# A later output projection, and two copies moved behind a product, in the core of an attention gradient kernel

## The chip, the cores and the metric

The kernel runs on one core of a Trainium2 chip. The metric is the device time of one execution in microseconds (us). Two kernels are compared by the ratio of the mean times of their fast runs of the same rounds on the same chip, with a 95% interval; this is not quite the ratio of the medians that are quoted beside it. A profile is that of a single execution, so its span differs by a few us from the median.

The engines are named as in the profiles: in this kernel PE does the matrix products (PEld is its loading of weights), ACT exponentials and copies, DVE and POOL element-wise work, and SP only issues DMAs. PSUM is the memory, in banks, that PE's products go to. The *granted clock* is the share of PE's full clock that the chip allowed, as the profile records it.

## The reference, cut to what matters

The reference returns the output and all input gradients of two attention blocks side by side: A is linear attention, B is softmax attention with 16 query heads of width 28 and a single key and value head. Only B's core matters here (S = 2048, D = 448):

```python
q = (x @ wq).reshape(B, S, H, Dh).transpose(0, 2, 1, 3)
k = x @ wk
v = x @ wv
p = softmax(einsum("bhqd,bkd->bhqk", q, k) * Dh ** -0.5)
o = einsum("bhqk,bkd->bhqd", p, v)
out_B = o.transpose(0, 2, 1, 3).reshape(B, S, H * Dh) @ wo   # the output projection
# ... and jax.vjp of all of it
```

## The kernel before

B's core computes forward and backward in one loop of 540 *units*. A block is 8 units: 256 queries of 2 heads against all 2048 keys. Eight blocks, 64 units, are a *group*: all heads of 256 queries. The scores S of unit u are computed together with the gradient product of unit u-16; the output o of a block is ready 8 units after the block starts, dQ 26 units after. Each engine follows the program order below; `due(u, lag)` gives the block that started `lag` units ago. Names in the code and the profiles: eT is the exponential of S and eN its transpose, which the product dv reads; onat is o by rows and oTq its transpose, which the output projection reads; qX is the copy of q that the product dk reads; a *cast* is the copy of the projection out of PSUM into the buffer that is stored.

```python
for u in range(NU + 28):
    w = u - 16
    if u == 14 or u % 64 == 32 and u < 448:          # qX of the next group, 16 loads by SP
        ...
        for a in range(4):
            for B in range(4):
                r0 = qc * 256 + 64 * B
                nc.sync.dma_start(qx[32 * a:32 * a + 32, B, :, :],
                                  qn_d[r0:r0 + 64, :].rearrange("(j s) c -> j s c", s=2))
    ...
    rows_SD(u, sp, dp)                                # PE: S and dP, into PSUM
    ...                                               # PE: transposes of o and dO into a spare bank
    if u % 64 in (4, 12) and u > 64:
        out_proj(u, spare)                            # PE: 4 matmuls that read oTq
    ... # ACT: eT = exp(S), first half
    ... # DVE: dsT = dP * eT, first half (the gradient product); ACT copies, POOL multiplies the other
    if (b := due(u, 10)) is not None:
        o_norm(b)
        do_o(b)
        if b % 8 == 7:                                # u % 64 == 2: o of a whole group is ready
            q_ = b // 8
            oTq[q_] = pp_.tile([P, 8, P], BF16, name="oTq", bufs=1)
            nc.sync.dma_start_transpose(oTq[q_][:, :, :], onat[q_]...)
    if u % 64 in (4, 12) and u > 64:
        out_store(u, spare)                           # DVE cast, then a store by SP
    ... # ACT: eT, second half; every odd unit SP issues the DMA transpose eN <- eT
    ... # PE: dk products (odd units); o, dq and dv products (even units); dv reads eN
    ... # DVE: stream transpose dsx <- dsT, row sum row_D
    if (b := due(u, 8)) is not None:                  # copy of o
        oTs[b] = pm_.tile([64, 256], F32, name="oTs", bufs=1)
        nc.vector.tensor_copy(out=oTs[b][:, :], in_=oq[0:64, 0:256])
    if (b := due(u, 26)) is not None:                 # copy of dQ
        ... nc.vector.tensor_scalar(out=qT_B[g]..., in0=oq[64:128, 0:256], scalar1=scale, ...)
```

The store takes its row tile from one fixed place, so two stores of a group share one buffer:

```python
def out_store(u, ps):
    i = 2 * (u // 64 - 1) + u % 64 // 8
    ot = flat(R3)[:, 5120:5120 + D]
    nc.vector.tensor_copy(out=ot, in_=ps[:, 0:D])
    nc.sync.dma_start(out0[i * P:(i + 1) * P, D:2 * D], ot)
```

## Time and profile before

| | before |
|---|---|
| median of 4 runs | 1224.02 us (1221.16 to 1226.29) |
| span of the profiled execution | 1216.1 us |
| block of 8 units with nothing in the way | 12.26 us |
| block with the first projection, groups 1 to 7 | 28.21, 22.65, 22.90, 22.72, 24.68, 23.87, 23.05 us |
| block with the second projection | 13.0 us |
| SP's lag at unit 64q+19, groups 1 to 7 | 0.03 us, in group 5 0.08 |

Block times are differences of start times of the first exponential of successive blocks in the trace. *SP's lag* is the time from the end of the second exponential of an odd unit, which completes eT, to the moment SP starts to issue the DMA transpose of that eT. Both are worked out from the start times in the timeline.

The windows view gives the busy time of each engine in a stretch without projections. ACT's 39.42 of 40 us is the fullest; DVE and PE follow closely:

```profile
core 0: us, PE busy (x) PEld busy (x) DVE busy (x) ACT busy (x) POOL busy (x), PEclk, DMA share, GB/s
400.00:440.00 40.00, 37.84 (x696) 16.85 (x689) 38.09 (x73) 39.42 (x79) 32.94 (x37) 1.00 0.94 168
```

The list of waits names who waited for whom (us in total, times, longest). PE's wait for the DMA that fills oTq is the cause in these four lines; the others are the engines that PE then held up:

```profile
ACT eT L826 <- PE dps L591: 91.2, 23, 15.9
DVE R L636 <- issue: 74.6, 8, 14.3
PEld L79 <- DMA oTq<-onat: 71.7, 8, 13.7
PE sps L79 <- DMA oTq<-onat: 69.5, 8, 13.5
```

The timeline of SP, which issues these DMAs, at one such stop (start, duration, instructions). The columns show SP issuing eN transposes until 699.84, though o of the group (onat) was written by DVE at 694.07; only then come the store of onat, the transpose into oTq and, once PE and DVE have worked again, the store of the output at 706.84:

```profile
689.24 10.50 SPq L850 DMA_TRANSPOSE eN<-eT  x4
699.84 0.85 SPq L721 DMA_DIRECT2D on_d<-onat  x1
700.74 1.28 SPq L841 DMA_TRANSPOSE oTq<-onat  x1
702.13 2.30 SPq L850 DMA_TRANSPOSE eN<-eT  x1
706.84 0.36 SPq L637 DMA_DIRECT2D out_dram<-R  x1
```

The chain that ended last, by line, has the copy of dQ as "DVE R L897" with 2%:

```profile
PE dk_acc L591 15%; PE agen L79 10%; PE oq L591 8%; PE dps L591 7%; PE sps L591 7%; DVE dsT L831 6%; PE dv_acc L591 5%; PE sps L79 5%; ACT eT L847 4%; DVE dsx L887 3%; ACT eT L826 3%; PE aacc L79 3%; DMA oTq<-onat 3%; DVE R L897 2%; PE dps L79 2%
```

### The profile page before, as it was taken

How to read it: one execution, taken by the hardware profiler on the slowest of the kernel's cores; microseconds unless marked ns; L12 is line 12 of the kernel's file. 1: busy time of each engine (PE TensorE's matmuls, PEld its weight loads, DVE VectorE, ACT ScalarE, POOL GpSimd, SP SyncE). 2: the span in 40 equal slices, each digit the busy share in tenths (PEclk: the TensorE clock that was granted, in tenths of full speed). 3: DMA queues.
4: the chain of work that ended last, by engine and by line, in shares of the span. 5: the costliest groups of instructions: out<-in, count | busy, mean ns of one | idle time of the engine just before them, and what ended most of it. 6: DMA issues, size and time to landing. Idle time of an engine off the chain costs nothing.

```text
span 1216.1 us, 38536 instructions
## 1 busy us (share of the span) xinstructions
PE 1069.1 (88%) x15379; PEld 487.8 (40%) x15388; DVE 903.3 (74%) x1733; ACT 875.0 (72%) x1724; POOL 700.7 (58%) x835
## 2 busy tenths in 40 slices
PE   7999989888985996999699879969996997899798
PEld 3555544333432443444244334424442443344344
DVE  7885400437995997899699879959996997899732
ACT  3543212457994997899699969959996998799421
POOL 9000230005883886688588858857885787688710
PEclk9999998986997999999899989989998999999899
DMA  9679894099999999899999999999999999999972
GB/s 254 126 138 180 179 207 112 6 194 188 169 189 172 172 166 199 153 161 178 175 176 166 187 159 170 176 170 163 161 190 164 167 170 198 153 173 169 221 153 73
DMA packets 684437, 202.92 MB, mean 167 GB/s; under 512 B 651232, under 2 KB 679392, under 8 KB 684256
## 3 DMA queue, kind: packets, MB, share of 16 engines
q1 hardware_dynamic: 673664, 190.26, 89.9%
q10 hardware_dynamic: 9312, 6.65, 1.9%
q0 software_dynamic: 1280, 3.55, 1.0%
q8 instruction: 120, 1.97, 0.6%
q14 instruction: 61, 0.50, 0.1%
HBM read 22.83 MB, written 15.03 MB: 31 GB/s over the span
## 4 chain that ended last, share of the span: by engine, by line
PE 64%; DVE 17%; ACT 9%; DMA 5%; SPq 3%; issue 2%; POOL 0%; ACTq 0%; DVEq 0%; POOLq 0%
PE dk_acc L591 15%; PE agen L79 10%; PE oq L591 8%; PE dps L591 7%; PE sps L591 7%; DVE dsT L831 6%; PE dv_acc L591 5%; PE sps L79 5%; ACT eT L847 4%; DVE dsx L887 3%; ACT eT L826 3%; PE aacc L79 3%; DMA oTq<-onat 3%; DVE R L897 2%; PE dps L79 2%
## 5 line engine op out<-in xcount | busy, mean ns | idle before, releaser
L834 POOL TENSOR_TENSOR dsT<-cp,eT 128x512 bf16<-128x512 bf16 x512 | 591.9, 1156 | 241.6 <-ACT cp L833 232.2
L826 ACT ACTIVATE eT<-sps 128x512 bf16<-128x512 f32 x512 | 307.3, 600 | 114.9 <-PE dps L591 91.2
L831 DVE TENSOR_TENSOR dsT<-dps,eT 128x512 bf16<-128x512 f32 x512 | 350.3, 684 | 41.8 <-PE dps L591 33.3
L887 DVE STREAM_TRANSPOSE dsx<-dsT 128x512 f32<-128x512 f32 x512 | 357.4, 698 | 1.1
L591 PEld LDWEIGHTS <-R 32*128 32x128 bf16 (+1 forms) x8192 | 203.4, 94 | 324.8 <-issue 274.0
L833 ACT ACTIVATE cp<-dps 128x512 bf16<-128x512 f32 x512 | 304.6, 595 | 19.8 <-PE dps L591 19.8
L847 ACT ACTIVATE eT<-sps 128x512 bf16<-128x512 f32 x512 | 310.5, 606 | 0.0
L591 PE MATMUL dps<-doT,R 32*128 32x256 bf16 x2048 | 255.7, 273 | 15.7 <-DVE dsT L831 14.5
L591 PE MATMUL dk_acc<-dsx,qX 32*32 32x512 bf16 x4096 | 269.3, 377 | 0.0
L591 PE MATMUL sps<-R,R 32*128 32x256 bf16 x2048 | 246.6, 279 | 18.5 <-ACT eT L826 4.4
L591 PE MATMUL oq<-eT,R 128*32 128x256 bf16 x2048 | 163.0, 283 | 0.0
L591 PE MATMUL oq<-dsT,R 128*32 128x256 bf16 x2048 | 162.6, 282 | 0.0
L591 PEld LDWEIGHTS <-qX 32*32 32x32 bf16 x4096 | 80.0, 89 | 114.7 <-issue 54.4
L591 PE MATMUL dv_acc<-eN,don 128*32 128x512 bf16 x1024 | 84.1, 398 | 0.5 <-DMA eN<-eT 0.5
L79 PE MATMUL sps<-R,oTq 128*128 128x448 bf16 x64 | 20.8, 464 | 69.5 <-DMA oTq<-onat 69.5
L636 DVE CAST R<-sps 128x448 bf16<-128x448 f32 x16 | 10.0, 624 | 74.9 <-issue 74.6
L521 DVE TENSOR_TENSOR osb<-R 32x512 bf16<-32x512 bf16 x4 | 1.7, 414 | 72.4 <-ACT R L518 72.4
L380 POOL MEMSET ga<- 64x448 bf16 x2 | 0.9, 469 | 90.7 <-PE agen L337 71.3
L79 PEld LDWEIGHTS <-R 128*128 128x128 bf16 (+1 forms) x416 | 34.1, 99 | 36.3 <-issue 12.0
L553 POOL MEMSET R<- 128x16 bf16 x1 | 0.2, 175 | 70.2 <-DVE R L552 70.2
L719 POOL TENSOR_TENSOR don<-R,rl 128x128 bf16<-128x128 bf16 x64 | 26.0, 406 | 21.0 <-DVE rl L711 21.0
L79 PEld LDWEIGHTS <-oTq 128*128 128x128 bf16 x64 | 5.9, 114 | 78.4 <-DMA oTq<-onat 71.7
(203 smaller groups left out, 994.6 us busy)
## 6 DMA issues: line engine op xcount, KB each, us to landing
qX<-qn_d SPq DMA_DIRECT2D x128, 64.0 KB
out_dram<-osb ACTq DMA_DIRECT2D x44, 112.0 KB
eN<-eT SPq DMA_TRANSPOSE x256
qn_d<-dsx SPq DMA_DIRECT2D x1, 2048.0 KB
on_d<-onat SPq DMA_DIRECT2D x8, 256.0 KB
xa<-in_A_x_dram SPq DMA_DIRECT2D x8, 224.0 KB
ga<-in_grad_out_dram SPq DMA_DIRECT2D x4, 448.0 KB
xa<-in_grad_out_dram POOLq DMA_DIRECT2D x4, 448.0 KB, 5.0
```

Source lines behind the costliest of these rows:

```text
L79: nc.tensor.matmul(out_ap, lhsT=lhsT, rhs=rhs, start=start, stop=stop, tile_position=(0, 0))
L521: nc.vector.tensor_tensor(out=sq[0:32, :], in0=kT[0:32, qc * 512:(qc + 1) * 512], in1=kT[0:32, qc * 512:(qc + 1) * 512], op=ALU.mult)
L591: nc.tensor.matmul(out, lhsT=lhsT, rhs=rhs, start=start, stop=stop, tile_position=pos, skip_group_check=True)
L636: nc.vector.tensor_copy(out=ot, in_=ps[:, 0:D])
L719: nc.gpsimd.tensor_tensor(out=dn[:], in0=dnv, in1=r_[:].to_broadcast([P, 2, 2, 32]), op=ALU.mult)
L826: nc.scalar.activation(out=et[:, u % 2, 0, :], in_=sp[0][:, :], func=ACT.Exp, scale=scale)
L831: nc.vector.tensor_tensor(out=dst[:, 0, :], in0=dp[0][:, :], in1=ew[:, w % 2, 0, :], op=ALU.mult)
L833: nc.scalar.activation(out=cp[:, :], in_=dp[1][:, :], func=ACT.Copy)
L834: nc.gpsimd.tensor_tensor(out=dst[:, 1, :], in0=cp[:, :], in1=ew[:, w % 2, 1, :], op=ALU.mult)
L847: nc.scalar.activation(out=et[:, u % 2, 1, :], in_=sp[1][:, :], func=ACT.Exp, scale=scale)
L887: nc.vector.transpose(out=dsx[b][:, tp, :, :, :].rearrange("p h t c -> p (h t c)").bitcast(F32), in_=dsT[y][:, :, :].rearrange("p h c -> p ...
L897: nc.vector.tensor_scalar(out=qT_B[g][64 * hp:64 * hp + 64, qc * 256:(qc + 1) * 256], in0=oq[64:128, 0:256], scalar1=scale, scalar2=None, ...
```

## The change

The intent is to read oTq long after its DMA was issued, and to let the gradient product, for which PE waits, go ahead of two DVE copies.

```diff
-            i = 2 * (u // 64 - 1) + u % 64 // 8
+            i = 2 * (u // 64 - 1) + (u % 64 == 24)          # in out_proj and in out_store
...
-                if u % 64 in (4, 12) and u > 64:
+                if u % 64 in (20, 24) and u > 64:
                     out_proj(u, spare)
...  (behind the gradient product of unit u:)
+                if (b := due(u, 9)) is not None:
+                    oTs[b] = pm_.tile([64, 256], F32, name="oTs", bufs=1)
+                    nc.vector.tensor_copy(out=oTs[b][:, :], in_=oq[0:64, 0:256])
+                if (b := due(u, 27)) is not None:
+                    ... nc.vector.tensor_scalar(out=qT_B[g]..., in0=oq[64:128, 0:256], ...)
...
-                if u % 64 in (4, 12) and u > 64:
+                if u % 64 in (20, 24) and u > 64:
                     out_store(u, spare)
...  (at the end of the unit:)
-                if (b := due(u, 8)) is not None:
-                    ...
-                if (b := due(u, 26)) is not None:
-                    ...
```

The second store now follows the first by 4 units instead of 8.

More of the change, by code (lines that the diff above doesn't have):

```diff
@@ L633, in out_store @@
         def out_store(u, ps):
-            i = 2 * (u // 64 - 1) + u % 64 // 8
+            i = 2 * (u // 64 - 1) + (u % 64 == 24)
             ot = flat(R3)[:, 5120:5120 + D]
@@ L834 @@
                     nc.gpsimd.tensor_tensor(out=dst[:, 1, :], in0=cp[:, :], in1=ew[:, w % 2, 1, :], op=ALU.mult)
+                if (b := due(u, 9)) is not None:
+                    oTs[b] = pm_.tile([64, 256], F32, name="oTs", bufs=1)
+                    nc.vector.tensor_copy(out=oTs[b][:, :], in_=oq[0:64, 0:256])
+                if (b := due(u, 27)) is not None:
+                    qc, pair, g, hp = blk(b)
+                    nc.vector.tensor_scalar(out=qT_B[g][64 * hp:64 * hp + 64, qc * 256:(qc + 1) * 256],
+                                            in0=oq[64:128, 0:256], scalar1=scale, scalar2=None, op0=ALU.mult)
                 if (b := due(u, 10)) is not None:
@@ L891 @@
                     row_D(b)
-                if (b := due(u, 8)) is not None:
-                    oTs[b] = pm_.tile([64, 256], F32, name="oTs", bufs=1)
-                    nc.vector.tensor_copy(out=oTs[b][:, :], in_=oq[0:64, 0:256])
-                if (b := due(u, 26)) is not None:
-                    qc, pair, g, hp = blk(b)
-                    nc.vector.tensor_scalar(out=qT_B[g][64 * hp:64 * hp + 64, qc * 256:(qc + 1) * 256],
-                                            in0=oq[64:128, 0:256], scalar1=scale, scalar2=None, op0=ALU.mult)
         gwo(60, 64)
```

## The prediction

> **What bounds the kernel now.** 900 of the profiled 1216 us are B's core (250 to 1165 us): 64 blocks of 8 units. Between first exponentials of successive blocks I measure 12.26 us where nothing is in the way. There ACT is busy 98.5%, DVE 95%, PE 95% (windows view, 400 to 440 us): all three nearly bind. In each group of 64 units the block with the first output projection takes 22.65 to 28.2 us, the one with the second 13.0.
>
> oTq is transposed by DMA after unit 64q+2 and read by PE at 64q+4. The wait list gives PE 69.5 us on it in 8 waits; ACT's 91 us before its exponentials and DVE's 74.6 us before the projection's cast are the same stops. The transpose lands in 3.6 us; the rest is the queue: SP (timeline) is 4 to 11 us behind there, because the 16 qX loads at unit 64q+32 hold it up by 8.7 us and it catches up 0.26 us per eN transpose. After each stop the clock is 0.5 for some 4 us, as the Trainium skill, "TensorE: Matmul & The Clock Gate", Part 1, says of an idle PE.
>
> **What the change does.** No work is added. Projections go to units 20 and 24, 27 us after the transpose is issued; its wait should vanish. Excess of the first block of groups 1 to 7 over 12.26: 82 us. Projections that do not wait keep 0.75 us each (as unit 12 now), so at most 77 us, plus some 4 of the 5.1 us wait in the tail.
>
> The copies of o (0.38 us) and dQ (0.43 us; 2% of the chain) stand on DVE before the gradient product of units 1 and 3 (of 8). Moved behind it, product 3 comes 0.4 us earlier, but the copy and the row sum then precede product 4, which starts when it does now; DVE has no gap from unit 1 to 5. I expect 12.26 to stay within 0.1: 0 from this part.
>
> **What takes some back.** In the stops SP catches up (lag 0.03 us after each). Without them SP needs per 64 units about 32 x 2.8 (eN gap when behind) + 8.6 (qX) + 2.2 (on_d, oTq) + 1.8 (stores) = 100.6 us, against 8 x 12.26 + 1.5 = 99.6 for the engines (estimates): the lag persists. The two stores share one SBUF buffer, now 4 units (6.1 us) apart: the second cast on DVE must wait for the first store, queued behind lagging transposes: about 1 us per group at a lag of 5, in group 1 (lag 9) about 5. I expect groups of about 101 us instead of 109 to 111.
>
> Group 1 -10, groups 2 to 6 -44, group 7 -9, tail -4: about -70 us from 1223.85.
>
> **Predicted: 1154 us, 8 in 10 within 1138 to 1170.** Faster by over 2%: 0.96; within 2%: 0.035; slower: 0.005.
>
> **What would show it.** PE's wait on oTq gone; blocks of 22 to 28 us become about 13; steady blocks 12.2 to 12.3; groups 100 to 102; SP's lag at unit 64q+20 3 to 10 us instead of near 0; a DVE wait before the second cast, largest (5 us) in group 1; dQ copy off the chain; clock nearer 1.0.
>
> **What would make it wrong.** If SP or DMA is slower than 2.8 us per transpose when never relieved, PE waits for eN at the dv product: groups of 103 or more, 1165 to 1175. A larger buffer wait does the same. If the copies do free the chain (12.26 falls to 12.0) and DMA keeps pace: 1135.

## The result, and the profile after

The changed kernel takes 1175.61 us in the median of 4 runs (1173.43 to 1180.85), against 1224.02: a ratio of 0.9612 (0.9574 to 0.965). The direction was right. The 48 us are less than the 70 foretold, and 1175.6 lies outside the stated range.

The profiled execution (span 1179.1 us) was the slowest of the four, while the one profiled before (1217.84 us in all) was faster than all four runs of its kernel; the two profiles therefore differ by only 37 us. 5.6 us of its length lie before B's core, which starts at 253.58 instead of 247.96 us; the kernels below, all with the same program there, start it between 247 and 257.

The wait for oTq is gone from the list of waits. In its place DVE, before its cast of the projection, waits for the DMA of the store, and PE waits for DVE:

```profile
ACT eT L826 <- PE dps L591: 51.1, 27, 10.0
DVE R L636 <- DMA out_dram<-R: 42.9, 8, 9.6
PE sps L591 <- DVE R L636: 30.9, 7, 8.9
```

The timeline of group 4 shows one such wait. First SP alone, which answers to the SP timeline of before; the 8 transposes are those of units it lagged behind with, and the store of the first projection comes after them:

```profile
697.12 23.17 SPq L857 DMA_TRANSPOSE eN<-eT  x8
720.38 0.70 SPq L637 DMA_DIRECT2D out_dram<-R  x1
721.19 2.31 SPq L857 DMA_TRANSPOSE eN<-eT  x1
```

Then DVE and PE from the same timeline (left out lines are other instructions). The first cast ended at 710.80. The store was issued 9.58 us later and landed (the last of its 16 semaphore updates in the trace) at 722.89, 2.51 us after that. The second cast, which must overwrite the buffer, sat idle for 6.52 us and started 0.12 us after the landing; PE's next score matmuls waited 5.87 us for that cast, as it frees their PSUM bank:

```profile
710.19 0.61 DVE L636 CAST R<-sps 128x448 bf16<-128x448 f32 x1
...
720.38 0.70 SPq L637 DMA_DIRECT2D out_dram<-R  x1
721.19 4.96 SPq L857 DMA_TRANSPOSE eN<-eT  x2
723.01 0.62 DVE L636 CAST R<-sps 128x448 bf16<-128x448 f32 x1 [6.52 <-DMA out_dram<-R]
723.55 0.70 DVE L894 STREAM_TRANSPOSE dsx<-dsT 128x512 f32<-128x512 f32 x1
723.69 0.39 PE L591 MATMUL sps<-R,R 32*128 32x256 bf16 x2 [5.87 <-DVE R L636]
```

Away from projections the engines are as full as before (two windows of 20 us), so the copies did not open a gap:

```profile
585.00:605.00 20.00, 19.09 (x358) 8.40 (x350) 19.10 (x38) 19.93 (x41) 16.22 (x18) 1.00 1.17 187
684.00:704.00 20.00, 19.12 (x355) 8.55 (x353) 19.23 (x36) 19.84 (x41) 16.37 (x19) 1.00 1.16 174
```

The chain that ended last still has the copy of dQ, now "DVE R L840", with 2%, and the store's DMA as a new member:

```profile
PE dk_acc L591 16%; PE agen L79 10%; DVE dsT L831 8%; PE sps L591 7%; PE dps L591 6%; PE oq L591 6%; DVE dsx L894 4%; ACT eT L854 4%; PE aacc L79 4%; PE sps L79 4%; PE dv_acc L591 3%; ACT eT L826 2%; PE dps L79 2%; DVE R L840 2%; DMA out_dram<-R 2%
```

Where the 37.0 us between the two profiled executions come from, against the prediction (all from first exponentials):

| part | predicted us | measured us |
|---|---|---|
| before the core | 0 | +5.6 |
| group 1 | -10 | -4.7 (114.77 to 110.07) |
| groups 2 to 6 | -44 | -28.6 (549.6 to 521.0) |
| group 7, its first seven blocks | -9 | -5.7 (97.5 to 91.8) |
| from the last exponential on | -4 | -3.6 (86.9 to 83.4) |

The block with the first projection is now 12.95 us long, as hoped. The block with the second is where the shortfall sits: 23.83, 16.34, 17.00, 20.07, 18.18, 17.83 and 17.75 us in groups 1 to 7, where 13.07 is what it takes with no wait (most groups of the run with two buffers, below). That is 39.5 us in all; the prediction had allowed about 11.

### The profile page after: what moved, and what is told of

Read it like the earlier page. It is cut to its first block, busy times and chain, and to the rows that moved or that the text cites. A ratio compares the mean times of both kernels' runs of the same rounds, so it can differ in the third digit from the quotient of the medians.

```text
span 1179.1 us, 38599 instructions
## 1 busy us (share of the span) xinstructions
PE 1072.2 (91%) x15379; PEld 487.1 (41%) x15388; DVE 902.6 (77%) x1733; ACT 877.4 (74%) x1724; POOL 696.6 (59%) x835
## 4 chain that ended last, share of the span: by engine, by line
PE 59%; DVE 21%; ACT 9%; issue 4%; DMA 4%; SPq 1%; POOL 1%; ACTq 0%; DVEq 0%; POOLq 0%
PE dk_acc L591 16%; PE agen L79 10%; DVE dsT L831 8%; PE sps L591 7%; PE dps L591 6%; PE oq L591 6%; DVE dsx L894 4%; ACT eT L854 4%; PE aacc L79 4%; PE sps L79 4%; PE dv_acc L591 3%; ACT eT L826 2%; PE dps L79 2%; DVE R L840 2%; DMA out_dram<-R 2%
## 5 line engine op out<-in xcount | busy, mean ns | idle before, releaser
L831 DVE TENSOR_TENSOR dsT<-dps,eT 128x512 bf16<-128x512 f32 x512 | 345.8, 675 | 37.9 <-PE dps L591 29.0
L591 PEld LDWEIGHTS <-R 32*128 32x128 bf16 (+1 forms) x8192 | 200.0, 94 | 350.7 <-issue 302.9
L591 PE MATMUL dk_acc<-dsx,qX 32*32 32x512 bf16 x4096 | 275.9, 385 | 0.0
L591 PE MATMUL dps<-doT,R 32*128 32x256 bf16 x2048 | 262.5, 277 | 9.5 <-DVE dsT L831 6.9
L591 PE MATMUL dv_acc<-eN,don 128*32 128x512 bf16 x1024 | 80.7, 385 | 0.8 <-DMA eN<-eT 0.8
L636 DVE CAST R<-sps 128x448 bf16<-128x448 f32 x16 | 9.9, 620 | 44.6 <-DMA out_dram<-R 42.9
L79 PE MATMUL agen<-R,R 128*128 128x448 bf16 x128 | 30.4, 369 | 3.2 <-DVE pk L227 1.9
L486 ACT ACTIVATE osb<-agen 128x448 bf16<-128x448 f32 x16 | 8.7, 542 | 28.9 <-DMA R<-xa 13.7
```

What stands on the lines that cost most here:

```text
L79: nc.tensor.matmul(out_ap, lhsT=lhsT, rhs=rhs, start=start, stop=stop, tile_position=(0, 0))
L486: nc.scalar.activation(out=ot[:], in_=ps[:, :], func=ACT.Copy)
L591: nc.tensor.matmul(out, lhsT=lhsT, rhs=rhs, start=start, stop=stop, tile_position=pos, skip_group_check=True)
L831: nc.vector.tensor_tensor(out=dst[:, 0, :], in0=dp[0][:, :], in1=ew[:, w % 2, 0, :], op=ALU.mult)
```

## The experiments

Ten runs of nine kernels were made (the last repeats the sixth). All were correct but one, which is told there. Each is compared with the kernel before on its own chip: 1222.08 us for the first four, 1224.41 for the next four and 1225.91 for the last two.

### Two buffers for the store

```diff
+        ot2 = pp_.tile([P, D], BF16, name="ot2", bufs=1)
-            ot = flat(R3)[:, 5120:5120 + D]
+            ot = ot2[:, :] if i % 2 else flat(R3)[:, 5120:5120 + D]
```

> The changed kernel, but the two stores of each group alternate between two SBUF buffers, so the second cast need not wait for the first store. Theory (the shortfall is the buffer wait, 42.9 us in 8 waits of the cast on the store's DMA): the cast's wait is gone, no other wait takes its place before group 3, SP's lag is no longer reset at unit 64q+24 and grows towards its limit, groups take about 100.5 us (102.9 to 110 after the change), 1143 us in all (1136 to 1152). Rival (SP and DMA cannot keep up at all, so the stop only moves): PE waits as long for eN at the dv product, groups stay at 103 or more, 1165 to 1176 us.

Measured: 1162.72 us, ratio 0.9517 (0.948 to 0.9554). The cast's wait for the store is gone, and the block of the second projection takes 13.07 to 13.27 us. But the gain over the changed kernel is only some 12 us (0.9612 less 0.9517, times 1224), not 32, because another wait came up where the changed kernel has at most 0.8 us of it:

```profile
PE dv_acc L591 <- DMA eN<-eT: 17.3, 11, 3.9
```

It stands in the block of units 48 to 55, which takes 19.36, 15.28, 13.04, 18.92, 14.25 and 15.09 us in groups 1 to 6 where 12.28 would do. SP's lag at unit 64q+47 is 12.2 to 17.7 us in those groups: no longer reset at unit 24, it has been raised by the 16 loads of qX at unit 32 (by 8.4 to 9.8 us from unit 31 to 33) and has not come down by then. Theory and rival each hold for a part: the buffer wait was real, and more than half of what its removal should have brought went into a wait for eN. Groups 2 to 6 take 102.5 us in the mean, not 100.5.

### Only the copies moved

The kernel before with the copies at their new places and the projections at units 4 and 12.

> The kernel before with only the copies of o and dQ moved (projections stay at units 4 and 12). Theory (the copies move from one place in a gapless DVE stretch to another): blocks without a projection 12.2 instead of 12.26 us, 1219 to 1224 us against 1224. Rival (the dQ copy's 0.43 us on the chain is freed in each of 64 blocks): blocks 11.9 to 12.0, 1200 to 1207 us.

Measured: 1224.32 us, ratio 1.0015 (0.9986 to 1.0045): no effect in the total. Blocks alternate between 12.28 and 12.16 us where the kernel before has 12.26. The rival (12.0 or less) is out.

### Only the projections moved

The kernel before with the projections at units 20 and 24 and the copies at their old places.

> The kernel before with only the projections moved to units 20 and 24 (copies stay). Theory: all of the gain comes from here, 1174 to 1180 us, with the same DVE wait of some 43 us for the store. Rival (the copies carry part of it): 1185 to 1195 us.

Measured: 1171.63 us, ratio 0.9589 (0.9554 to 0.9624), which overlaps the interval of the whole change. DVE waits 38.2 us for the store. So the projections carry all of the gain that can be told from noise, and bring the new wait with them. The median is 2 us under the lower edge of the expected range.

### The store issued by another engine

```diff
-            nc.sync.dma_start(out0[i * P:(i + 1) * P, D:2 * D], ot)
+            nc.gpsimd.dma_start(out0[i * P:(i + 1) * P, D:2 * D], ot)
```

> The changed kernel, one buffer, but the two stores are issued from POOL's queue, so that they do not stand behind the transposes in SP's program order. Theory (the store is late because SP issues it after the transposes it lags with, not because the write is slow): the cast's wait is gone although the buffer is shared, 1140 to 1156 us, near the run with two buffers. Rival (the DMA engines' backlog delays the write whoever issues it): the wait stays above 25 us and the time at 1165 or more.

Measured: 1164.84 us, ratio 0.9526 (0.9495 to 0.9558). With one buffer, the cast's wait falls from 42.9 to 1.1 us, as the view of the store's line shows (it lists POOL's DMA instructions, who waited for them, and the time to landing):

```profile
L637 POOL DMA_DIRECT2D out_dram<-R x16: 540/581/615, 394.1 to 1121.6; - x16
...
  DVE R L636: 1.1, 1
...
DMA to landing us min/median/max: 2.0/3.7/6.5
```

POOL issued the first store of each group 0.30 to 0.42 us after the cast, where SP in the changed kernel needed 4.5 to 12.7 us. The write still took 2.0 to 6.5 us to land, but that mostly fits between the two casts. So the store was late because of its place in SP's program order behind the transposes. The rival (a wait above 25 us) is out by the wait; the time, 1164.8 us, would have suited it as well. The time missed the range of the theory, 1140 to 1156, for the reason found above: PE waits 16.6 us for eN.

### Four loads of qX instead of sixteen

```diff
                     for a in range(4):
-                        for B in range(4):
-                            r0 = qc * 256 + 64 * B
-                            nc.sync.dma_start(qx[32 * a:32 * a + 32, B, :, :],
-                                              qn_d[r0:r0 + 64, :].rearrange("(j s) c -> j s c", s=2))
+                        nc.sync.dma_start(qx[32 * a:32 * a + 32, :, :, :].rearrange("j b s c -> j b (s c)"),
+                                          qn_d[qc * 256:qc * 256 + 256, :].rearrange(
+                                              "(b j s) c -> j b (s c)", b=4, s=2))
```

> The changed kernel with one buffer, but qX of a group is loaded by 4 DMAs of 256 KB instead of 16 of 64 KB. Theory (SP's lag at the store comes from the 8.7 us that SP takes to issue the 16 loads, 0.46 us each, not from the DMA engines): SP is held up by 2 to 3 us instead of 8.7, its lag has gone before unit 64q+20, the cast's wait falls from 42.9 us to under 15 (most of it in group 1), 1140 to 1156 us. Rival (the loads' bytes hold up the DMA engines as long): lag and wait as before, 1168 to 1178.

Measured: 1147.66 us, ratio 0.9374 (0.9327 to 0.9421). SP's lag at unit 64q+19 is 1.3 to 3.3 us in groups 2 to 7 (5.0 to 9.1 in the changed kernel), and only 7.5 us of waiting for the store remain, most of it in group 1, where the lag of the core's start is not yet worked off (6.8 us):

```profile
DVE R L636 <- DMA out_dram<-R: 7.5, 2, 5.3
```

The same bytes (512 packets of 2 KB either way) in a quarter of the instructions do away with most of the lag at that unit. But the rival is only half out. SP is busy with the loads for 1.8 to 3.3 us instead of 8.0 to 11.0; the transpose right behind them, however, now takes 4.1 to 5.2 us to issue instead of 1.8 to 2.9. Over both, from unit 31 to 35, the lag rises by 4.4 us instead of 8.0 (mean of groups 1 to 6). So the number of instructions accounts for nearly half of what the loads cost SP; what the other half is was not tested.

### Both together

Two buffers and four loads.

> Two buffers for the store and 4 loads of qX together. Theory (what is left with two buffers, 17.3 us of PE waiting for eN in the block of units 48 to 55, is the same lag of SP): both waits gone, groups of 99.3 us, 1132 to 1146 us. Rival (the DMA engines themselves need over 100 us per group): PE still waits for eN by 10 us or more, 1155 or more.

Measured: 1139.88 us, ratio 0.9308 (0.9266 to 0.9351). Groups take 99.3 to 99.6 us, but for group 5 with 102.4, where PE waited once for eN, 1.9 us. From 565 to 653 us the windows view shows ACT busy 85.69 of 88 us (97%), across two projections:

```profile
565.00:653.00 88.00, 83.58 (x1516) 37.22 (x1516) 83.62 (x158) 85.69 (x171) 70.92 (x78) 1.00 1.19 187
```

SP is still behind, by 6.6 to 14.9 us at the seven units of each of groups 1 to 6 that were looked at: with nothing left to reset it, the lag creeps up, from 9.3 us at unit 47 of group 0 to 13.9 in group 5. The wait of group 5 was for the eN of unit 39, where the lag was 14.7 us; in the other groups it was 14.3 or less there. This is no sharp limit: with two buffers alone, PE waited 1.6 us at a lag of 13.7. In the repeat of this kernel, below, the lag at unit 47 stayed at 7.6 to 11.7 us and no such wait came.

### The second projection at unit 28

`(20, 24)` becomes `(20, 28)`: twice the distance between the stores, one buffer.

> The changed kernel with the second projection at unit 28 instead of 24, so 8 units (12.2 us) between the casts that share the buffer. Theory (the wait is lag + issue + landing - distance): each of the 8 waits is about 6 us shorter, so most are gone and about 5 to 10 us of 42.9 remain; but SP's lag is then not reset, and PE waits for eN instead as with two buffers: 1160 to 1168 us. If there were no such second limit: 1140.

Measured: 1165.7 us, ratio 0.9516 (0.9469 to 0.9562). The result was wrong: the last group's second projection would fall in unit 540, after the loop's end, so 128 rows of the output were never written (NaN in the first output, the others correct). The time therefore lacks one projection in the tail. Up to there the loop does all its work: the cast still waits 19.5 us in 7 waits, instead of 42.9, and PE waits 4.0 us for eN. The wait fell by less than the 6 us each that were foretold: with a lag that is no longer reset so early, the first store is issued 10.3 to 13.3 us after its cast instead of 6.2 to 12.7. Distance helps less than taking away the lag.

### The kernel before with four loads

> The kernel before, only with 4 loads of qX instead of 16. Theory (the stop for oTq is SP's lag of 4 to 6 us plus 4 us for the transpose and SP's own work): lag near 0 at unit 64q+2, stops of 4 to 5 us instead of 8 to 9 in groups 2 to 6, first blocks of 18 to 19 us instead of 22.7, 1190 to 1205 us. Rival (the stop is the transpose's own latency): 1219 to 1226.

Measured: 1196.39 us, ratio 0.9784 (0.9728 to 0.984): faster, clear of noise, though whether by 2% is not. The stop for oTq fell from 69.5 to 46.8 us of PE's waiting:

```profile
PE sps L79 <- DMA oTq<-onat: 46.8, 8, 9.9
```

SP's lag at unit 64q+1 is 0.0 to 2.4 us in groups 2 to 7 (4.0 to 5.9 in the kernel before), and first blocks of groups 2 to 6 take 20.0 us in the mean instead of 23.4. They had been expected at 18 to 19. So the lag made about a third of the old stop; the rest is what it takes, even with SP nearly on time, to get oTq two units after o is ready.

### The copies once more, without the waits

The kernel with two buffers and four loads, once with the copies at their old places and once as above, 5 rounds each on one chip.

> Two buffers and 4 loads of qX, projections at units 20 and 24, but the copies of o and dQ at their old places. Theory (the copies' move is worth what the blocks show, 12.26 against 12.28 and 12.16 in turn, so 0.04 us in each of 64 blocks): 2 to 4 us slower than the same kernel with the copies moved, blocks of 12.26 us. Rival (with the big waits gone the dQ copy's place on the chain counts in full): 15 us or more slower, blocks of 12.26 against 12.0.

> The kernel with two buffers and 4 loads of qX once more, on the same chip as the one with the old places of the copies: 1136 to 1143 us, groups of 99.3 us, at most one short wait for eN. Under the theory it beats the other by 2 to 4 us, which may be within noise; under the rival by 15.

Measured: 1140.47 us, ratio 0.9316 (0.9281 to 0.9352) with the old places; 1138.3 us, ratio 0.9279 (0.9252 to 0.9307) with the new ones. Groups 1, 4, 5 and 6 take 99.74 and 99.31 us (in 2 and 3 the difference is 0.5), and neither kernel has a wait for eN or for the store in its list. The profiles thus give the copies 0.43 us per group, 3.4 us in all. The totals agree with that but do not prove it, as the intervals overlap. A worth of 15 us is out.

The last kernel has the lowest ratio found: 0.9279 of the kernel before, where the change alone is 0.9612. Its lead over the one with the old places is not shown.

## Why the prediction was right or wrong, point by point

- **"its wait should vanish": right.** PE's 69.5 us on oTq are gone, and blocks with the first projection went from 22.65 to 28.2 us down to 12.95.
- **"0 from this part" (the copies): right.** Moving them alone gives 1.0015, and the blocks alternate between 12.28 and 12.16, within the 0.1 us allowed. That the dQ copy would leave the chain was wrong: it is still there with 2%. The timeline shows why it costs the same. In a block before, the products of units 2, 3 and 4 (of 8) start at 619.42, 621.63 and 623.03 us; in one after, at 705.92, 707.52 and 709.58. Product 3 comes 0.6 us earlier, but the copy then stands before product 4, and from 2 to 4 it is 3.61 us before and 3.66 after.
- **A new DVE wait before the second cast, from the shared buffer behind SP's lag: the mechanism right, the size wrong. This is the step that failed:** "about 1 us per group at a lag of 5, in group 1 (lag 9) about 5". Two terms of it were mis-sized.
  - *The wait for a given lag.* It was taken as lag - 4 us. From the measured blocks it is lag - 1.6 us in the mean of groups 1 to 7 (for instance 7.0 us at a lag of 9.12 in group 4). The distance between the casts was right: 6.75 us from start to start, 6.1 without the cast; lag - 4 thus leaves 2.1 us for all else. The store was issued 0.8 us later than the lag alone says in the mean, and from 0.3 us earlier to 2.0 later (12.73, 6.51, 6.56, 9.58, 7.46, 6.22 and 7.02 us after its cast at lags of 12.11, 5.23, 5.62, 9.12, 6.95, 6.53 and 4.99). It then took 2.3 to 3.6 us to land, 2.6 in the mean. (In the kernel before, where SP had just caught up, the same stores took 1.7 to 3.8 us, 2.3 in the mean, so a busy queue adds little.) The sum is about lag - 2.6. The last 1.0 us is not in DVE's wait, but in the blocks; it fits the halved clock after each stop (Restarts, below), though no run separates it.
  - *The lag.* It was taken as 5 us, and 9 in group 1, which is what the kernel before has at unit 64q+1 (5.0 in the mean of groups 2 to 6, 9.3 in group 1). At unit 64q+19 it was 6.7 in the mean of groups 2 to 6, and 12.1 in group 1. The trace shows the way there: 5.8 us (10.2) at unit 64q+1; 7.8 (13.4) at 64q+3, after SP issued the store of onat and the transpose into oTq; then only a slow fall. In the kernel before, the stop at unit 4 wiped that rise out. SP's gap between eN issues when over 1 us behind is not the reason: 2.86 us in the mean, 2.85 before.
  - Together the waits cost 39.5 us instead of about 11. With lag - 4, the measured lags would have given 22.6; so 11.5 us of the error come from the lag and 17 from the wait for a given lag. That is the shortfall: 28.5 us too little allowed, of which some 4 us came back because groups without waits (99.3 to 99.6) are shorter than had been set (101 with 1 us of wait).
- **"the lag persists": right, and it stands behind both stops.** SP's time per group had been estimated at 100.6 us against 99.6 for the engines. With the buffer wait removed the groups ran at 102.5 us and PE waited for eN, as foretold under "what would make it wrong" (there as groups of 103 or more). Both stops are one lag seen by two different readers, so removing one alone brought 12 us. Cutting about half of its source (four loads) and one of its readers (two buffers) brought groups of 99.3 us.
- **Restarts.** The Trainium skill, "TensorE: Matmul & The Clock Gate", Part 1, says that PE's clock is halved after some 3.4 us of idling. The trace agrees in kind: around the 5.87 us stop shown above the windows view gives a granted clock of 0.50 from 722 to 727 us (it fell some 2.7 us after PE's last matmul) and of 1.00 from 728, and the first score matmuls of 32x256 stand at 0.39 us where the timeline otherwise has 0.28. So a stop costs more than its wait, which the estimates by block include and the wait list does not.

What stays open: why SP's gap per transpose, when behind, is near 2.85 us (the issue instruction alone lasts 2.48 us in the median before), and so how much of it is SP's and how much the DMA engines'. No run here separates the two. That the transpose behind four large loads takes 4.1 to 5.2 us to issue, against 1.8 to 2.9 behind sixteen small ones, shows only that its length depends on what was issued before it.

## What to carry to other kernels

A stop that is taken away may have been the moment at which a lagging queue caught up: before counting the whole stop as gain, ask what that queue's lag will be without it, and list every reader and every buffer that will then see the lag. A store issued in program order behind a lagging stream is late by that stream's lag, and a single buffer turns that into a wait of the engine that fills it. Here fewer, larger DMA instructions on the queue that lags were worth more than a second buffer (0.9374 against 0.9517), and the two together more than either.

## What the Trainium skill lacked or had wrong

- "DMA: Bandwidth & Descriptors", section "Issuing engines are not separate DMA queues", says that issuing from several engines only saves the time the sequencer needs to initiate a DMA, "which is usually small relative to the DMA itself". Here it was not small: a transpose kept SP for 2.48 us in the median, and behind several of them a 112 KB store waited 4.5 to 12.7 us to be issued and landed 2.3 to 3.6 us later; from POOL it was issued 0.30 to 0.42 us after its cast.
- The same page, section "Anatomy of one DMA", gives about 2.0 us of fixed cost (for DMAs from POOL) and calls it nearly constant. From POOL, beside SP's stream of transposes, the store of 112 KB took 2.0 to 6.5 us to land, 3.7 in the median. (From SP, for which the section does not speak, it was 1.7 to 3.8 us where SP had caught up and 2.3 to 3.6 where it was behind.) The page says elsewhere that less load on HBM lowers this cost, but has no figure for a DMA beside such a stream.
- "Perfetto Trace Analysis", section "What 'DMA-bound' means", names the issuing sequencer as a bound and advises large descriptors. Here the rows moved stayed 2 KB long and only the number of instructions fell, 16 to 4 per group; SP's time on them fell from 8.0 to 11.0 us to 1.8 to 3.3 us, though the transpose behind them took 2.7 us longer in the mean, and the kernel's time fell from 1175.6 to 1147.7 us. That section does not tell the number of DMA instructions from the size of descriptors.
- No page was found that says how long the issuing sequencer is busy with one DMA transpose of an SBUF tile on this chip ("DMA: Bandwidth & Descriptors" has cycles only for unnamed "previous generations", in a part on a later chip, and without the size of a tile); for 128x2048 elements of bf16 it is 2.48 us in the median before the change (1.3 to 8.7), and one is issued per 2.85 us when SP is behind.
